# Spreading weight sums, moving stores to ScalarE's queue and low halves to VectorE in a clustered-attention and MLP kernel

## The chip, the cores and the metric

One core of one Trainium2 chip. The time is device microseconds (us) of one execution; lower is better. TensorE multiplies, VectorE (DVE), ScalarE (ACT) and GpSimd (POOL) do elementwise work, SyncE (SP) issues DMAs and computes nothing.

## The reference

Float32 attention whose keys and queries see each other only in the same cluster, and on its output a small mixing MLP:

```
q_assign = argmax(q_n @ c_n.T); k_assign = argmax(k_n @ c_n.T)     # 16 centroids a head
attn = softmax(where(q_assign == k_assign, q @ k.T / 8, -1e9)) @ v # batch 4, heads 8, seq 768, dim 64
x = attn as (4, 768, 512)
u = x + (x^T @ U @ V)^T                                            # rank 32 along seq
out = u + relu(u @ w_ch1) @ w_ch2                                  # 512 -> 2048 -> 512
```

## The kernel before

**Precision.** A float32 operand is split into a high part, rounded to the fast matmul type (a copy, called hi, on ScalarE), and a low part, x - hi (a subtraction, on POOL or DVE). A product is three matmuls: hi x hi, hi x lo, lo x hi. So every operand passes through ScalarE and then POOL or DVE before TensorE can use it.

**Seven products.** The large matrix products use a 2x2 block scheme with seven block products (`products`, line 840) in place of eight. It needs sums of the blocks of weights and activations: s1 to s4 of a weight, t1 to t4 of an activation. `factors`: a11, a12, a22 are raw blocks (three, 768 columns), the four s are sums (1024 columns).

**Stages, in order of time.** To about 444 us: attention. Then the MLP, three kinds of stage:

- *First stage*, 444 to 738 us: 16 groups g (0 to 15), each one batch b and one pair k of eight slices of the hidden layer. Runs: batch 0 k 0 to 3, batch 1 k 0 to 7, batch 0 k 4 to 7. A group has 42 matmuls of 384 columns (`product`, lines 853 to 855, combined on DVE at 861), a Relu on ScalarE (893) and its low half on DVE (891), and 36 matmuls of 512 columns of the second GEMM with plain weights (`gemm2`, 1044 to 1046). On the side the group prepares the next group's weights: `add_w` (819, POOL), `split_w` (829 hi on ScalarE; 827 low, on POOL until group 12's weights, then on DVE), `split_w2` (838 hi; 836 low on POOL); and it joins raw 64-bit weight words (`convert`, 713 to 724; DVE lines 218 to 221).
- *Product stages* of batches 2 and 3 (738 to 809 and 885 to 944): eight groups of 42 matmuls each (g 16 to 31). The weights are read back from memory (`stage_w`, 936) and split (`split_staged`: hi 945, low 943). The Relu results stay in the buffers `h_*` (`relu_home`).
- *Step stages* of batches 2 and 3 (809 to 885, 944 to 1015): the second GEMM, now also by seven products. 56 steps n2 = 8 p + k (product p 0 to 6, k 0 to 7), each six matmuls (`product2`, 994 to 996). A block is eight steps of one p. The activations are split on the way: `split_h` (hi 923, low 921), two k at a time into a ring of four places; `add_h` (914, POOL) makes t1, t2, t4; in batch 2's step stage the u of batch 3 is prepared as well (797 on POOL, 803 and 804). `combine2` (1004 to 1017) adds the blocks, `output` transposes (1027), adds u (1030) and stores (1034). The w2 factors are loaded by `load_w2` (the line of the helper `copy_rows`, 261) into 14 slots; slots 11 to 13 hold the fourth ring place until step 48.

For the step stages, the first stage writes to memory: `keep_sums` (927), the sums of the first weights, 512 KB; `keep_w2` (953), three pieces of 256 KB of split w2; `sums_w2`, per k, eight stages: load 512 KB (963), four sums (968, POOL), hi (970, ScalarE), low (972, POOL), store 1 MB (974). `sums_w2` works in the tile `turned`, which is needed for the blocks of u again from group 14 on.

**Order.** Nothing is scheduled at run time. `at(time, fn, ...)` gives each piece a planned time in units (one product each: a group of the first or the product stage is 7 units, a step is 1); the plan is sorted, and every engine and every DMA queue runs its pieces in that order, waiting on semaphores. So a piece that waits holds what is behind it on its engine, DMA issues too. M0 is the start of group 0, M1 = M0 + 112 that of group 16. Nearly all DMAs are issued by SP.

The placement of the sums, lines 1237 to 1240, and the slots, 976 and 977:

```
for k in range(NK):
    at(M0 + 7 * (k + 4 if k < 4 else k + 8) + 5, keep_w2, k)
    for stage, step in enumerate(phase["sums"]):
        at(M0 + 7 * (k + 5) + step, sums_w2, k, stage)
slots = [n2 % 11 if n2 < 6 * NK else 7 + n2 % NK % 7 for n2 in range(7 * NK)]
slots = {2: slots, 3: slots[:-1] + [0]}
```

Of the kernel before, what the change touches and what calls it, by code (L numbers as in the profile page):

```python
# [51 lines left out]
NK = NF // 2  # L52
# [73 lines left out]
    "sums":    (-2.5, -0.3,  0.1,  0.5,  0.9,  1.4,  1.6,  3.2),  # L126
    "open":    4.5,
    "keep_sums": 0.5,
    "stage":   (-5.0, -3.5),
    "split_w": ( 0.3,  1.2,  1.3,  3.0),  # L130
    "relu":    ( 4.6,  5.6,  6.6,  6.5,  7.4),
    "t1":      10.6,
    "split_h": (-3.8, -2.8),
    "t2":      ( 4.0,  1.8),
    "t4":      (14.5,  2.0),
    "output":  (( 1.2,  1.7,  3.0), ( 2.2,  2.7,  4.0)),
# [26 lines left out]
def clustered_attention_moe(ctx: ExitStack, tc: tile.TileContext, qk, v, cen, moe_U, moe_V, w, out):  # L163
# [752 lines left out]
    def split_h(p, kk, low):  # L916

        x = homes_h[products[p][1]][:, 2 * kk:2 * kk + 2].rearrange("p k q -> p (k q)")
        hi, lo = (ring[kk][:, m] for m in range(2))
        if low:  # L920
            (nc.gpsimd if (4 * p + kk) % 3 == 2 else nc.vector).tensor_sub(lo, x, hi)
        else:
            nc.scalar.copy(hi, x)

    def keep_sums(k):

        nc.sync.dma_start(out=s_scr[k], in_=sums_w)
# [10 lines left out]
    def split_staged(g, part, low):  # L938

        x = staged[g, part].rearrange("p (i c) -> p i c", c=256)  # L940
        hi, lo = (combos[pairs[g][2] % 2][:, 3 * part:3 + 4 * part, m] for m in range(2))
        if low:
            nc.gpsimd.tensor_sub(lo, x, hi)  # L943
        else:
            nc.scalar.copy(hi, x)
# [3 lines left out]
    def keep_w2(k):  # L949

        w2 = live["w2", k % 2]
        for i, (f, c) in enumerate(((0, 0), (1, 0), (1, 256))):
            copy_rows(nc.sync, w2_scr[k][:, i], w2[:, :, f, c:c + 256])
# [3 lines left out]
    def sums_w2(k, stage):  # L957

        x = flat[:, 0:1024]
        pieces = flat[:, 1024:3072].bitcast(F32R).rearrange("p (i m c) -> p i m c", i=4, m=2)  # L960
        if stage == 0:
            assert {(k, 1, 0), (k, 1, 1)} <= stored
            nc.sync.dma_start(out=x, in_=w_scr[k][1])
# [5 lines left out]
        elif stage == 5:  # L969
            nc.scalar.copy(pieces[:, :, 0], x.rearrange("p (i c) -> p i c", i=4))  # L970
        elif stage == 6:
            nc.gpsimd.tensor_sub(pieces[:, :, 1], x.rearrange("p (i c) -> p i c", i=4), pieces[:, :, 0])
        else:
            copy_rows(nc.sync, w2_scr[k][:, 3:7], pieces)

    slots = [n2 % 11 if n2 < 6 * NK else 7 + n2 % NK % 7 for n2 in range(7 * NK)]
    slots = {2: slots, 3: slots[:-1] + [0]}

    def load_w2(b, n):

# [40 lines left out]
    def output(b, p, o, stage):  # L1021
# [223 lines left out]
    def weights_phase(g, m):  # L1245

        for part in range(2):
            at(m + phase["stage"][part], stage_w, g, part)
            for low in range(2):
                at(m + phase["split_w"][2 * part + low], split_staged, g, part, low)  # L1250

    for r, b in enumerate((2, 3)):
# [37 lines left out]
        if r == 0:  # L1290
# [8 lines left out]
            weights_phase(ng + NK, m0 + 14 * NK - 7.8)  # L1299
# [36 lines left out]
```

## Time and profile before

| | |
|---|---|
| time, median of 2 runs | 1022.21 us (1021.65 to 1022.78) |
| profiled execution | 1022.64 us, span 1020.8 us |
| mean granted TensorE clock | 0.975 |
| busy in the span: TensorE, DVE, ScalarE, POOL | 944.5, 768.6, 464.3, 723.4 us |
| DMA moved | 183.14 MB, mean 179 GB/s |

In the rows an engine is PE, DVE, ACT, POOL or SP; a trailing q is its queue of waits and DMA issues. L853 is line 853. "out<-in" names tiles. "<-POOL x L836" is what ended the idle time before. Matmuls overlap, so a busy TensorE is not one at its peak; its granted clock is a share of the full 2.4 GHz, 0.5 being the lower level, 1.2 GHz.

### The profile page before, as it was taken

The page shows a single profiled execution, that of the slowest core. Times are in us where ns is not written, and L with a number is a line of the kernel's source. Part 1 is how long each engine was busy: PE and PEld are TensorE (multiplying, and loading weights), DVE is VectorE, ACT ScalarE, POOL GpSimd, SP SyncE. Part 2 cuts the span into 40 slices and gives each one's busy share as a digit, 9 for nine tenths or more (in the row PEclk, how much of TensorE's full clock was granted, in tenths as well). Part 3 has the DMA queues.
Part 4 walks back from the last instruction along what each step waited for, and adds up shares of the span by engine and source line. Part 5 has one row for each costly group of instructions (what it writes and reads, how often), then busy time and mean ns, then how long its engine had stood idle before and what let it go on. Part 6 is the DMA issues. An engine that isn't in the chain of part 4 may idle for free.

```text
span 1020.8 us, 14867 instructions
## 1 busy us (share of the span) xinstructions
PE 944.5 (93%) x5098; PEld 759.6 (74%) x5098; DVE 768.6 (75%) x1217; ACT 464.3 (45%) x680; POOL 723.4 (71%) x467
## 2 busy tenths in 40 slices
PE   8799999999999999999989779979998969999996
PEld 5466666666667667658877667968898869899895
DVE  5798988778887877568785687665878887687763
ACT  6355555565555545544342433323345543155430
POOL 6467776788678879985787898883647694366950
PEclk8899999999999999999999899999999998999998
DMA  8556656575656674047468665589486956795675
GB/s 204 131 141 165 168 148 187 154 193 145 190 148 183 164 165 104 1 73 228 157 239 293 224 256 183 203 285 259 130 195 164 228 157 194 208 201 173 197 212 126
DMA packets 169646, 183.14 MB, mean 179 GB/s; under 512 B 110426, under 2 KB 119252, under 8 KB 168548
## 3 DMA queue, kind: packets, MB, share of 16 engines
q1 hardware_dynamic: 169056, 182.04, 64.0%
q8 instruction: 40, 0.66, 0.3%
q14 instruction: 34, 0.28, 0.1%
q10 hardware_dynamic: 516, 0.16, 0.1%
HBM read 112.72 MB, written 41.42 MB: 151 GB/s over the span
## 4 chain that ended last, share of the span: by engine, by line
PE 60%; POOL 12%; DVE 11%; DMA 6%; SPq 4%; issue 4%; ACT 3%; ACTq 0%; POOLq 0%; DVEq 0%
PE o_ps L616 12%; PE ps_max L569 6%; PE st L593 6%; PE st L595 5%; PE ps_h L853 3%; PE ps_h L855 3%; PE ps_h L854 3%; SPq L786 3%; POOL h_left L914 3%; PE y L1046 2%; PE y L1045 2%; PE y L1044 2%; POOL turned L968 2%; PE z L995 2%; PE z L994 2%
## 5 line engine op out<-in xcount | busy, mean ns | idle before, releaser
L608 POOL TENSOR_TENSOR T<-T,pr 128x768 f32<-128x768 f32 x120 | 222.7, 1856 | 52.6 <-DVE T L608 30.9
L571 DVE TENSOR_REDUCE m<-ps_max 128x1 f32<-128x384 f32 x372 | 186.7, 546 | 44.9 <-PE ps_max L569 43.4
L598 ACT ACTIVATE pr<-st 128x768 f32<-128x768 f32 x186 | 148.9, 812 | 74.9 <-PE st L595 63.8
L616 PE MATMUL o_ps<-pr,vt 128*64 128x384 f32 x768 | 131.4, 491 | 0.6 <-DMA vt<-in_v 0.2
L853 PE MATMUL ps_h<-arena,combos 128*128 128x384 f32 x352 | 119.8, 340 | 6.9 <-DVE rw_g L861 3.4
L855 PE MATMUL ps_h<-arena,combos 128*128 128x384 f32 x352 | 118.8, 337 | 3.6 <-POOL combos L943 3.6
L569 PE MATMUL ps_max<-arena 128*128 128x384 f32 x372 | 114.8, 375 | 7.5 <-DMA arena<-ohT 5.6
L854 PE MATMUL ps_h<-arena,combos 128*128 128x384 f32 x352 | 118.9, 338 | 0.5 <-DVE arena L804 0.5
L616 PEld LDWEIGHTS o_ps<-pr,vt 128*64 128x64 f32 x768 | 52.4, 137 | 66.6 <-issue 60.8
L593 PE MATMUL st<-arena 128*128 128x384 f32 x372 | 100.1, 350 | 1.3 <-ACT pr L598 1.3
L569 PEld LDWEIGHTS ps_max<-arena 128*128 128x128 f32 x372 | 67.9, 191 | 41.4 <-issue 15.2
L595 PE MATMUL st<-arena 97*128 97x384 f32 x372 | 95.8, 339 | 0.0
L608 POOL TENSOR_TENSOR T<-pr 128x768 f32<-128x768 f32 x30 | 56.5, 1883 | 46.4 <-ACT pr L598 46.4
L1046 PE MATMUL y<-w,hl 128*128 128x512 f32 x192 | 77.8, 405 | 8.1 <-DVE hl L891 7.9
L1045 PE MATMUL y<-w,hh 128*128 128x512 f32 x192 | 77.1, 401 | 6.7 <-POOL w L836 6.7
L853 PEld LDWEIGHTS ps_h<-arena,combos 128*128 128x128 f32 x352 | 66.5, 189 | 14.6 <-issue 4.6
L593 PEld LDWEIGHTS st<-arena 128*128 128x128 f32 x372 | 65.1, 189 | 16.4 <-issue 7.3
L1044 PE MATMUL y<-w,hh 128*128 128x512 f32 x192 | 75.6, 394 | 1.4 <-ACT hh L893 1.4
L893 ACT ACTIVATE hh<-c 128x768 fp32r<-128x768 f32 x32 | 27.0, 845 | 98.8 <-DVE c L861 97.7
L855 PEld LDWEIGHTS ps_h<-arena,combos 128*128 128x128 f32 x352 | 66.5, 189 | 5.2 <-POOL combos L943 5.2
L854 PEld LDWEIGHTS ps_h<-arena,combos 128*128 128x128 f32 x352 | 66.5, 189 | 4.8 <-DVE arena L804 1.0
L595 PEld LDWEIGHTS st<-arena 97*128 97x128 f32 x372 | 68.4, 190 | 0.0
(212 smaller groups left out, 2177.3 us busy)
## 6 DMA issues: line engine op xcount, KB each, us to landing
combos<-w_scr SPq DMA_DIRECT2D x112, 256.0 KB
R<-in_qk SPq DMA_DIRECT2D x32, 384.0 KB
arena<-arena SPq DMA_DIRECT2D x64, 192.0 KB
arena<-arena SPq DMA_DIRECT2D x31, 384.0 KB
late_rw<-in_w SPq DMA_DIRECT2D x20, 512.0 KB
u<-u_scr SPq DMA_DIRECT2D x96, 96.0 KB
w_scr<-turned SPq DMA_DIRECT2D x8, 1024.0 KB
rw<-w_scr SPq DMA_DIRECT2D x15, 512.0 KB
```

The costliest lines, as they stand in the source:

```text
L569: nc.tensor.matmul(ps[:, 0:HS], x1[:, 0, g // 2, g % 2, t * P:(t + 1) * P], x1[:, 1, h, g % 2, :], start=True, stop=True)
L571: nc.vector.reduce_max(live["m2", i][:, h, u:u + 1], ps[:, 0:HS], axis=AX.X)
L593: nc.tensor.matmul(st[:, j, 0:HS], x1[:, 1, hk, j, ks], x1[:, 0, h, j, :], start=True, stop=False)
L595: nc.tensor.matmul(st[:, j, 0:HS], x2[0:97, 1, hk, j, ks], x2[0:97, 0, h, j, :], start=False, stop=True)
L598: nc.scalar.activation(pr, st[:, :, 0:HS], AF.Exp, scale=SCALE)
L608: eng.tensor_add(T, live["p", i, h, 0] if c == 1 else T, live["p", i, h, c])
L616: nc.tensor.matmul(o_ps[64 * j:64 * j + 64, 0:HS], vv[:, c, j, :], pr[:, j, :], start=(c == 0), stop=(c == NT - 1))
L853: nc.tensor.matmul(ps, ah[:, d], oh[:, d], start=(d == 0), stop=False)
L854: nc.tensor.matmul(ps, ah[:, d], ol[:, d], start=False, stop=False)
L855: nc.tensor.matmul(ps, al[:, d], oh[:, d], start=False, stop=(d == 1))
L1045: nc.tensor.matmul(y, hh[:, f, ts], w2[:, 1, f, :], start=False, stop=False)
L1046: nc.tensor.matmul(y, hl[:, f, ts], w2[:, 0, f, :], start=False, stop=(g in lasts and f == 1))
```

## The change

- `sums_w2` no longer stands in groups 5 to 12, one per group, but in groups 5, 7, 8, 10, 11, 13, 14 and 15. Its load is planned four units ahead of the group (2.5 before), its store at 5.0 (3.2 before). For k of 5 and up it works in two tiles of the raw-weight conversion (`late_rw`, `late_g`), and its low half is on DVE.
- `keep_w2` moves by about five units, `keep_sums` by one.
- The DMAs of `keep_sums`, `keep_w2`, the load and the store of `sums_w2`, and the stores of `output` except the last ones of batch 3 are issued by ScalarE. That is 8 + 24 + 8 + 8 + 56 = 104 issues.
- `split_staged`: the low half of part 0 (768 columns) goes from POOL to DVE. `split_h`: all 24 low halves of a step stage on DVE (16 before); planned two units earlier. The stores of `output` are planned two units later.
- Slots of the last block: 7, 8, 9, 10, 6, 11, 12, 13 in both batches (before 7 to 13, and then 7, or 0 in batch 3).
- The first weights of batch 3's product stage are loaded 0.8 units later; the second part is split at -2.6 and -1.5 units before that stage in place of -6.5 and -4.8.

```
 phase = {
-    "sums":    (-2.5, -0.3,  0.1,  0.5,  0.9,  1.4,  1.6,  3.2),
+    "sums":    (-4.0, -0.3,  0.1,  0.5,  0.9,  1.4,  1.6,  5.0),
+    "sums_at": (5, 7, 8, 10, 11, 13, 14, 15),
-    "keep_sums": 0.5,
+    "keep_sums": 1.5,
-    "split_w": ( 0.3,  1.2,  1.3,  3.0),
+    "split_w": ( 0.1,  1.3,  1.1,  2.2),
-    "split_h": (-3.8, -2.8),
+    "split_h": (-5.8, -4.8),
-    "output":  (( 1.2,  1.7,  3.0), ( 2.2,  2.7,  4.0)),
+    "output":  (( 1.2,  1.7,  5.0), ( 2.2,  2.7,  6.0)),
...
-            (nc.gpsimd if (4 * p + kk) % 3 == 2 else nc.vector).tensor_sub(lo, x, hi)
+            nc.vector.tensor_sub(lo, x, hi)
...
-        nc.sync.dma_start(out=s_scr[k], in_=sums_w)
+        nc.scalar.dma_start(out=s_scr[k], in_=sums_w)
...
-            nc.gpsimd.tensor_sub(lo, x, hi)
+            (nc.gpsimd if part else nc.vector).tensor_sub(lo, x, hi)
...
-            copy_rows(nc.sync, w2_scr[k][:, i], w2[:, :, f, c:c + 256])
+            copy_rows(nc.scalar, w2_scr[k][:, i], w2[:, :, f, c:c + 256])
...
-        x = flat[:, 0:1024]
-        pieces = flat[:, 1024:3072].bitcast(F32R).rearrange("p (i m c) -> p i m c", i=4, m=2)
+        if k < 5:
+            x, pieces = flat[:, 0:1024], flat[:, 1024:3072]
+        else:
+            pieces, x = (t.rearrange("p h n -> p (h n)").bitcast(F32) for t in live["late_w"][0:2])
+        pieces = pieces.bitcast(F32R).rearrange("p (i m c) -> p i m c", i=4, m=2)
...
-            nc.sync.dma_start(out=x, in_=w_scr[k][1])
+            nc.scalar.dma_start(out=x, in_=w_scr[k][1])
...
-            nc.gpsimd.tensor_sub(pieces[:, :, 1], x.rearrange("p (i c) -> p i c", i=4), pieces[:, :, 0])
+            (nc.gpsimd if k < 5 else nc.vector).tensor_sub(pieces[:, :, 1], x.rearrange("p (i c) -> p i c", i=4), pieces[:, :, 0])
...
-            copy_rows(nc.sync, w2_scr[k][:, 3:7], pieces)
-    slots = [n2 % 11 if n2 < 6 * NK else 7 + n2 % NK % 7 for n2 in range(7 * NK)]
-    slots = {2: slots, 3: slots[:-1] + [0]}
+            copy_rows(nc.scalar, w2_scr[k][:, 3:7], pieces)
+    slots = [n2 % 11 if n2 < 6 * NK else (7, 8, 9, 10, 6, 11, 12, 13)[n2 % NK] for n2 in range(7 * NK)]
...
+            queue = nc.sync if b == B - 1 and p == 6 else nc.scalar
...
-                nc.sync.dma_start(out=dst[j, :, 12 * side:12 * side + 12, 2 * half + o, :], in_=x[32 * j:32 * j + 32])
+                queue.dma_start(out=dst[j, :, 12 * side:12 * side + 12, 2 * half + o, :], in_=x[32 * j:32 * j + 32])
...
-        at(M0 + 7 * (k + 4 if k < 4 else k + 8) + 5, keep_w2, k)
+        at(M0 + 7 * (k + 5 if k < 4 else k + 9) + 2.9, keep_w2, k)
-            at(M0 + 7 * (k + 5) + step, sums_w2, k, stage)
+            at(M0 + 7 * phase["sums_at"][k] + step, sums_w2, k, stage)
...
-            weights_phase(ng + NK, m0 + 14 * NK - 7.8)
+            weights_phase(ng + NK, m0 + 14 * NK - 7, (-0.6, 0.5, 4.4, 5.5))
```

## Rows read from the trace of the kernel before

**Rows 1.** the page: TensorE's busy time, and the chain that ended last
```profile
PE 944.5 (93%) x5098; PEld 759.6 (74%) x5098; DVE 768.6 (75%) x1217; ACT 464.3 (45%) x680; POOL 723.4 (71%) x467
...
PE 60%; POOL 12%; DVE 11%; DMA 6%; SPq 4%; issue 4%; ACT 3%; ACTq 0%; POOLq 0%; DVEq 0%
```

**Rows 2.** windows: us, busy (instructions) per engine, granted clock, DMA share, GB/s
```profile
533.12:689.54 156.42, 133.08 (x625) 116.29 (x625) 105.33 (x123) 54.34 (x70) 133.95 (x97) 0.95 0.70 244
689.54:705.19 15.65, 15.65 (x79) 14.07 (x79) 7.91 (x12) 5.34 (x7) 6.24 (x6) 1.00 1.06 228
689.54:737.97 48.43, 47.50 (x236) 41.99 (x235) 34.04 (x46) 17.23 (x22) 24.24 (x16) 1.00 0.74 184
750.40:808.77 58.37, 53.92 (x306) 52.63 (x305) 46.39 (x74) 27.72 (x43) 37.88 (x21) 1.00 0.84 192
808.77:847.42 38.65, 29.13 (x145) 27.85 (x145) 35.63 (x25) 15.56 (x22) 36.10 (x16) 0.90 0.62 172
873.39:885.10 11.71, 9.21 (x49) 8.24 (x49) 5.62 (x9) 1.88 (x2) 4.22 (x2) 1.00 1.00 287
944.09:976.02 31.93, 27.67 (x146) 26.40 (x146) 25.84 (x21) 12.47 (x18) 29.63 (x14) 0.95 0.68 194
976.02:1000.98 24.96, 24.96 (x145) 24.96 (x145) 11.91 (x17) 7.54 (x9) 7.30 (x4) 1.00 0.67 200
1000.98:1014.90 13.92, 10.71 (x49) 9.41 (x48) 5.42 (x12) 0.00 (x0) 0.00 (x0) 0.88 0.59 150
```

**Rows 3.** POOL, 533.12 to 689.54, grouped: busy us, mean ns | idle before, releasers
```profile
L968 POOL TENSOR_TENSOR turned<-turned 128x256 f32<-128x256 f32 x32 | 29.8, 932 | 8.5 <-DMA turned<-w_scr 6.6
L972 POOL TENSOR_TENSOR turned<-turned 128x1024 fp32r<-128x1024 f32 x8 | 19.3, 2417 | 9.3 <-ACT turned L970 9.3
```

**Rows 4.** TensorE's waits, 533.12 to 689.54: us in total, times, longest
```profile
PE y L1046 <- DVE hl L891: 7.9, 3, 4.2
PE y L1045 <- POOL w L836: 6.7, 3, 3.4
```

**Rows 5.** TensorE's waits, 808.77 to 847.42
```profile
PE z L995 <- POOL combos L921: 5.2, 1, 5.2
PE z L995 <- POOL arena L921: 4.3, 3, 2.7
```

**Rows 6.** TensorE's waits, 873.39 to 885.10
```profile
PE z L994 <- DMA combos<-w_scr: 2.5, 3, 1.4
```

**Rows 7.** TensorE's waits, 1000.98 to 1020.80
```profile
PE z L994 <- DMA combos<-w_scr: 3.2, 2, 1.6
```

**Rows 8.** tile mT, DMA issues on ScalarE's queue: ns min/median/max, first, last
```profile
L261 ACTq DMA_DIRECT2D arena<-mT x17: 677/732/1287, 36.3 to 417.8; - x17
```

**Rows 9.** timeline of SP, 890 to 1021
```profile
998.94 1.97 SPq L1034 DMA_DIRECT2D out_y<-u  x4
1001.01 2.79 SPq L261 DMA_DIRECT2D combos<-w_scr  x6
```

**Rows 10.** groups of instructions on ScalarE, 533.12 to 689.54
```profile
L970 ACT CAST turned<-turned 128x1024 fp32r<-128x1024 f32 x8 | 8.4, 1052 | 38.7 <-POOL turned L968 38.7
```

**Rows 11.** timeline of DVE, 682 to 740: start us, us, instruction
```profile
683.29 2.82 DVE L827 TENSOR_TENSOR combos<-sums_w,combos 128x1024 fp32r<-128x1024 f32 x1
...
733.33 1.21 DVE L827 TENSOR_TENSOR combos<-sums_w,combos 128x1024 fp32r<-128x1024 f32 x1
```

**Rows 12.** timeline of DVE, 795 to 890
```profile
839.48 5.02 DVE L921 TENSOR_TENSOR arena<-h_t,arena 128x768 fp32r<-128x768 f32 x2
...
857.42 0.95 DVE L921 TENSOR_TENSOR arena<-h_left,arena 128x768 fp32r<-128x768 f32 x1
```

**Rows 13.** timeline of POOL, 795 to 890
```profile
834.48 6.74 POOL L914 TENSOR_TENSOR h_left<-h_left 128x768 f32<-128x768 f32 x3
841.18 2.51 POOL L921 TENSOR_TENSOR combos<-h_left,combos 128x768 fp32r<-128x768 f32 x1
```

**Rows 14.** timeline of ScalarE, 846 to 858
```profile
854.92 0.84 ACT L923 CAST arena<-h_left 128x768 fp32r<-128x768 f32 x1 [0.56 <-PE z L996]
```

More of the change, by code (lines that the diff above doesn't have):

```diff
@@ L971, in sums_w2, with load_w2 @@
         elif stage == 6:
-            nc.gpsimd.tensor_sub(pieces[:, :, 1], x.rearrange("p (i c) -> p i c", i=4), pieces[:, :, 0])
+            (nc.gpsimd if k < 5 else nc.vector).tensor_sub(pieces[:, :, 1], x.rearrange("p (i c) -> p i c", i=4), pieces[:, :, 0])
         else:
-            copy_rows(nc.sync, w2_scr[k][:, 3:7], pieces)
-    slots = [n2 % 11 if n2 < 6 * NK else 7 + n2 % NK % 7 for n2 in range(7 * NK)]
-    slots = {2: slots, 3: slots[:-1] + [0]}
-    def load_w2(b, n):
+            copy_rows(nc.scalar, w2_scr[k][:, 3:7], pieces)
+    slots = [n2 % 11 if n2 < 6 * NK else (7, 8, 9, 10, 6, 11, 12, 13)[n2 % NK] for n2 in range(7 * NK)]
+    def load_w2(n):
         p, k = divmod(n, NK)
-        slot = slots[b][n]
+        slot = slots[n]
         copy_rows(nc.sync, combos[slot // 7][:, slot % 7], w2_scr[k][:, factors2.index(products[p][0])])
     def product2(b, p, k, *tiles):
-        slot = slots[b][NK * p + k]
+        slot = slots[NK * p + k]
         w2 = combos[slot // 7][:, slot % 7]
@@ L1237, in clustered_attention_moe, with weights_phase @@
     for k in range(NK):
-        at(M0 + 7 * (k + 4 if k < 4 else k + 8) + 5, keep_w2, k)
+        at(M0 + 7 * (k + 5 if k < 4 else k + 9) + 2.9, keep_w2, k)
         for stage, step in enumerate(phase["sums"]):
-            at(M0 + 7 * (k + 5) + step, sums_w2, k, stage)
+            at(M0 + 7 * phase["sums_at"][k] + step, sums_w2, k, stage)
     M1 = M0 + 7 * ng
     at(M1 + phase["open"], open_phase)
-    def weights_phase(g, m):
+    def weights_phase(g, m, steps=phase["split_w"]):
         for part in range(2):
@@ L1249, in weights_phase @@
             for low in range(2):
-                at(m + phase["split_w"][2 * part + low], split_staged, g, part, low)
+                at(m + steps[2 * part + low], split_staged, g, part, low)
     for r, b in enumerate((2, 3)):
@@ L1265, in clustered_attention_moe @@
             p, k = divmod(n2, NK)
-            before = [x for x in range(n2) if slots[b][x] == slots[b][n2]]
-            free = before[-1] + 1 if before else 0 if slots[b][n2] > 6 else -7
-            at(m + max(free, n2 - 10.7, 6 * NK if slots[b][n2] > 10 else -7) + 0.3 + 0.02 * n2, load_w2, b, n2)
+            before = [x for x in range(n2) if slots[x] == slots[n2]]
+            free = before[-1] + 1 if before else 0 if slots[n2] > 6 else -7
+            at(m + max(free, n2 - 10.7, 6 * NK if slots[n2] > 10 else -7) + 0.3 + 0.02 * n2, load_w2, n2)
             if b < B - 1 or p < 6:
```

## The prediction

> **What bounds the kernel now.** I read the page first [rows 1]: TensorE is busy 93% of the span, but the chain that ended last is only 60% TensorE; POOL and DVE have 23% of it. So TensorE is the floor, and what the change can touch is the time in which it stands or runs at the lower clock. Next I cut the second half of the span into its stages [rows 2]. One full group of the first MLP stage (7 products and its second GEMM, 78 matmuls) takes 15.65 us when nothing is late. Groups 5 to 12 take 156.42 us for eight, where 8 x 15.65 = 125.2 would do: 31.2 lost. Those are the groups in which the sums of the second weights are made, one per group. Three blocks of eight steps in the last product stage take 24.96 us undisturbed (1.04 us a step); the first three blocks take 38.65 for batch 2 and 31.93 for batch 3: 13.7 and 7.0 lost. The last block takes 11.71 and 13.92 against 8.32: 3.4 and 5.6 lost. All of that is 61 us; the rest of the span the change hardly reaches.
>
> Then I asked in each stage which wait ends last. In groups 5 to 12 POOL is busy 134 of 156 us, and most of its idle time is waiting in mid-chain for ScalarE's cast or a load [rows 2, 3]: its order of work is a loop that is longer than TensorE's. TensorE waits for POOL's low half of w2 and for DVE's low half of the activations [rows 4]. In the step stages it waits for POOL's low halves alone [rows 5], in the last blocks for loads of w2 factors [rows 6, 7].
>
> **The change, part by part.** The sum is made against the profiled execution, 1022.64 us (span 1020.8 and 1.84 around it); the median of the runs is 0.4 below it.
>
> *A. Sums spread, groups 5 to 12.* One sum costs POOL 29.8/8 + 19.3/8 = 6.1 us of work and (8.5 + 9.3)/8 = 2.2 us of waiting in it [rows 3], 8.35 together. Eight stand in these groups before, five after (5, 7, 8, 10, 11): 3 x 8.35 = 25 us leave POOL's loop, 156.4 becomes 131.4, just above TensorE's 125.2. The load four units ahead may also hide the 6.6 us of load waits. Against it: ScalarE now issues DMAs. On its queue one took 0.73 us (0.68 to 1.29) for 6 KB [rows 8]; SP's six 256 KB loads took 0.47 each [rows 9]. I take 0.73, the row on that engine. With three pieces of w2, a load, a store and sometimes the first sums that is 5 x 0.73 = 3.7 us in a group, where ScalarE already waits 38.7 us for POOL in eight groups [rows 10]. A new wait comes with them: the store of the pieces stands until the subtraction is done, and behind it the second Relu, for which DVE's low half and then TensorE wait. Where two sums follow each other (7 and 8, 10 and 11) POOL is still late, and I charge the issues fully: 2 x 3.5 = 7. Gain 25 - 7 = 18; bounds 8 (late in most groups) and 31.
>
> *B. Groups 13 to 15 get three sums.* POOL is busy 24 of 48.4 us there [rows 2], so 3 x 3.7 fit. The subtraction goes to DVE: 1.21 us, or 2.82 beside a busy POOL [rows 11]. The DMA share is 0.74 at 184 GB/s; three loads of 0.5 MB and three stores of 1 MB more make some 270, below the 287 that the last block of batch 2 moved [rows 2]. Cost 2; bounds 0 and 3 x 2.82 = 8.5.
>
> *C. Product stages, batches 2 and 3.* Seven or eight low halves of 768 columns a stage go from POOL to DVE, 0.95 each [rows 12] on a DVE that is busy 46.4 of 58.4 us [rows 2]; POOL's remaining work holds DVE up less. I take 0, bounds -3 (DVE is nearly full) and +1.
>
> *D. Low halves in the steps, all on DVE and two steps earlier.* The rows show a price that depends on the other engine: DVE's 768-column subtraction took 0.95 us with POOL idle and 5.02 for two with POOL working, and POOL's own 2.25 to 2.51 [rows 12, 13]. They take turns, one each per 2.5 us. In the 5.2 us wait, POOL made the needed half only after three differences of h, 834.48 to 841.22 [rows 5, 13]. After the change, steps 3 to 25 (22.9 us) hold for batch 2 ten POOL instructions (4 + 4 differences, 2 of u) and 18 of DVE (12 halves, 4 of u, 2 output additions): ten turns of 2.5 and eight at 0.95 are 32.6 us. A half is planned 4.8 steps ahead of its use, 5.0 - 0.95 = 4.0 us of cover: 32.6 - 22.9 - 4.0 = 5.7 stays lost of 13.7. (The same reckoning before, 14 and 14 with 2.8 steps of cover, gives 10 of the 13.7; the granted clock of 0.90 is in the rest.) Gain 8, bounds 4 and 13.7. Batch 3 has no u to split: eight turns and six at 0.95 are 25.7, covered. I take 5.5 of 7.0, since eight output stores (8 x 0.73 = 5.8 us) now stand between ScalarE's casts, and wait there for DVE's addition; bounds 3 and 7.
>
> *E. Last block, batch 2.* SP no longer stands at the output stores, so the loads go out when the slot is free: up to 3 of the 3.4 [rows 6]. But the second part of the next stage's first weights is now cast at step 53.4 behind four stores: 2.9 + 1.05 (cast [rows 10]) + 2.4 (POOL, 1024 columns [rows 3]) from step 53.1 ends near step 59.2, and is used at step 58. Net gain 1.5, bounds -1 and 3.
>
> *F. Last block, batch 3.* SP issued six loads only at 1001.01, after stores at 998.94 [rows 9], and TensorE waited 3.2 us in two waits, with a clock of 0.88 in this block [rows 2, 7]. Now only three slots are still tied to the end of block five. Gain 3, bounds 1 and 4.5.
>
> Here a rule speaks against the change: the Trainium skill, "DMA: Bandwidth & Descriptors", section "Issuing engines are not separate DMA queues", says that DMAs of all issuing engines run on the same 16 engines, and that a second issuer saves only the time to initiate. The row shows the loads held back at SP itself, before any transfer. By the rule E and F would lose their gains and the sum would be 6 less; by the row they stay.
>
> Sum: 18 - 2 + 0 + 8 + 5.5 + 1.5 + 3 = 34, and 1022.6 - 34 = 989.
>
> **The rivals.** *All stalls go.* POOL's loop stays under TensorE's and ScalarE hides its issues: A 28, B 0, D 21, E 3, F 4.5 make 56.5: 966. For it: a group without a sum runs at 15.65 [rows 2]; against it: five sums still leave POOL's loop at 131.
>
> *The lead is not there, and the loads stay late.* ScalarE's casts already wait for TensorE to free the ring [rows 14], so a cast cannot come earlier. Then D is only the difference in price: POOL's 1024 columns cost twice DVE's (2.42 and 1.21 [rows 3, 11]), so each of some nine halves saves about 0.9, 8 in place of 13.5, and E and F give -1.5 and 3 at most: 18 - 2 + 8 + 1.5 = 25.5, 997. This is the case in which part of the change does not do what it says. By the skill's rule on issuing engines it would be 1000.
>
> *ScalarE takes POOL's place.* Its 104 new issues are 76 us, and each in-order wait for POOL or DVE holds casts and Relus behind it. A falls to 10 and D to 6, the rest is nothing: 1022.6 - 14 = 1008.
>
> *Slower.* The 48 issues of the first stage (48 x 0.73 = 35 us) lie wholly on the way from cast to Relu to TensorE, with POOL's loop as the wait behind them, and A gives nothing: 1022.6 + 35 - 13 = 1045. It decides from 34/11 = 3 us of delay a group on; ScalarE is busy 54 of 156 us there by its casts, so most issues should find it idle.
>
> **How the numbers follow.** Forecast 0.50, all go 0.13, no lead 0.12, ScalarE 0.20, slower 0.05. The time is 989. The forecast's own bounds reach from about 975 to 1003; with the near parts of the others the range is 969 to 1012. A measurement of this kernel tells 2% (20 us, 1001.8) from no change. Faster: nearly all of the first three, 0.73; the same: ScalarE's case and a little of the forecast, 0.22; slower 0.05.
>
> **What would show it.** Right: groups 5, 6, 8, 9, 11 and 12 nearer 15.7 us, with POOL idle in 6, 9 and 12; no low half of h on POOL (line 921); first three blocks near 30 and 26 us; loads for the last block issued before the previous block ends. Wrong: ScalarE's queue waiting for POOL ahead of a Relu, DVE's queue as the releaser in the product stages, the DMA share near 1 in groups 13 to 15, or TensorE standing at the third product of batch 3's first group.

## The result, and the profile after

The changed kernel took 1011.88 us (1011.86 to 1011.91, 2 runs) against 1022.21: ratio 0.9899, 95% interval 0.9856 to 0.9942. The forecast was 989 (969 to 1012): the sign was right, the gain of 10.3 us is a third of the 34 forecast. The profiled execution has a span of 1009.5 us, 11.3 less than before. Cut at the first matmul of each stage, the two traces give:

| stage (term of the forecast) | before | after | gain | forecast |
|---|---|---|---|---|
| up to group 5 | 533.1 | 530.4 | 2.7 | none |
| groups 5 to 12 (A) | 156.4 | 143.7 | 12.7 | 18 |
| groups 13 to 15 (B) | 48.4 | 62.1 | -13.7 | -2 |
| product stage, batch 2 (C) | 70.8 | 73.6 | -2.8 | 0 |
| blocks 1 to 4, batch 2 (D) | 48.0 | 44.8 | 3.2 | 8 |
| last block, batch 2 (E) | 11.7 | 8.3 | 3.4 | 1.5 |
| product stage, batch 3 (C) | 59.0 | 62.0 | -3.0 | 0 |
| blocks 1 to 4, batch 3 (D) | 40.3 | 35.6 | 4.7 | 5.5 |
| last block, batch 3 (F) | 13.9 | 9.9 | 4.0 | 3 |

The gains add up to 11.2 us. Each stage length is of one execution. The start of group 5 lies between 528.8 and 533.5 us in 16 other kernels with nearly the same code up to there, so most of a difference in it can be scatter. But group 4, the last ahead of it, took 19.4 us before and 17.4 in after and in all 16 others: 2.0 of the first 2.7 come with the change, and the forecast had no term for them. It is not the queue, since the 17.4 stay with the early DMAs on SP; what else it is was not parted.

The page of after, its busy line and the engines of the chain that ended last, beside [rows 1]:

```profile
PE 943.9 (93%) x5098; PEld 757.4 (75%) x5098; DVE 781.2 (77%) x1251; ACT 463.8 (46%) x680; POOL 656.8 (65%) x433
...
PE 64%; DVE 13%; POOL 7%; DMA 6%; issue 4%; ACT 3%; SPq 2%; ACTq 1%; POOLq 0%; DVEq 0%
```

POOL lost 67 us of work, DVE took up 13, and the chain has a little less POOL and SP in it. Such a line does not say where 11 us came from. The windows of after do (columns as in [rows 2]): groups 5 to 12; groups 13 to 15; of these, 13, 14 and 15 alone; blocks 1 to 3, block 4 and the last block of batch 2; blocks 1 to 3, block 4 and the last block of batch 3:

```profile
530.44:674.11 143.67, 131.97 (x625) 115.34 (x624) 101.03 (x122) 52.07 (x67) 117.53 (x84) 0.96 0.70 240
674.11:736.20 62.09, 51.92 (x236) 44.84 (x235) 40.61 (x49) 21.62 (x27) 35.70 (x28) 0.93 0.70 215
674.11:689.75 15.64, 15.64 (x79) 13.91 (x79) 10.12 (x13) 5.86 (x7) 9.43 (x10) 1.00 0.99 252
689.75:712.70 22.95, 17.95 (x79) 15.16 (x79) 14.06 (x22) 7.32 (x9) 10.29 (x10) 0.93 0.76 239
712.70:736.20 23.50, 18.33 (x80) 15.77 (x79) 16.42 (x16) 8.44 (x11) 15.99 (x10) 0.89 0.45 168
809.81:839.25 29.44, 26.69 (x145) 24.77 (x145) 29.44 (x22) 14.36 (x20) 24.60 (x11) 1.00 0.68 207
839.25:854.56 15.31, 10.33 (x49) 9.69 (x49) 11.11 (x14) 5.34 (x7) 2.11 (x1) 0.89 0.66 167
871.20:879.52 8.32, 8.32 (x49) 8.32 (x49) 4.91 (x10) 1.02 (x2) 0.00 (x0) 1.00 1.01 316
941.49:966.55 25.06, 25.06 (x146) 24.95 (x145) 25.03 (x20) 11.25 (x16) 21.83 (x9) 1.00 0.76 242
966.55:977.06 10.51, 8.83 (x49) 8.27 (x49) 7.74 (x12) 3.88 (x5) 0.00 (x0) 1.00 0.88 230
993.70:1003.58 9.88, 9.31 (x49) 8.03 (x48) 5.41 (x11) 0.00 (x0) 0.00 (x0) 1.00 0.71 150
```

Group 13 takes the undisturbed 15.6, although a sum stands in it; 14 and 15 take 7.3 and 7.9 us more than that. In blocks 1 to 3 of both batches DVE is busy all the time, and block 4 is slow, which it was not before. TensorE's waits in groups 13 to 15 (0.9 us in all before), and then the longest of DVE and of ScalarE there (columns: us in total, times, longest):

```profile
PE ps_h L854 <- DVE rw_g L862: 5.2, 2, 4.0
PE ps_h L854 <- DVE c L862: 4.6, 2, 4.1
PE y L1050 <- DVE hl L892: 0.4, 1, 0.4
...
DVE turned L793 <- DMA u<-u_scr: 6.9, 2, 5.6
DVE late_rw L976 <- ACT late_rw L974: 6.3, 3, 4.6
...
ACT late_rw L974 <- POOL late_g L972: 7.9, 2, 5.6
```

Read upward, the longest of these are two chains. In group 15 POOL makes the differences of a late sum late; ScalarE's cast (L974) stands 5.6 us at them; DVE's low half (L976) stands 4.6 us at the cast; behind it in DVE's line is the combination (L862) for which TensorE waits 4.1 us. In group 14 DVE's transposes of u stand 5.6 us at their loads, and behind them is the combination for which TensorE waits 4.0 us. The waits are 10.2 us; the rest of the loss goes with the clock: after the two long waits TensorE is granted the lower of its levels, 1.2 in place of 2.4 GHz, for a part of the group (mean 0.93 and 0.89 in these rows, 1.00 in the undisturbed one).

### The profile page after: what moved, and what is told of

The parts are those of the page before. It is cut to its first block, busy times and chain, and to the rows that moved or that the text cites. A ratio compares the mean times of both kernels' runs of the same rounds, so it can differ in the third digit from the quotient of the medians.

```text
span 1009.5 us, 14837 instructions
## 1 busy us (share of the span) xinstructions
PE 943.9 (93%) x5098; PEld 757.4 (75%) x5098; DVE 781.2 (77%) x1251; ACT 463.8 (46%) x680; POOL 656.8 (65%) x433
## 4 chain that ended last, share of the span: by engine, by line
PE 64%; DVE 13%; POOL 7%; DMA 6%; issue 4%; ACT 3%; SPq 2%; ACTq 1%; POOLq 0%; DVEq 0%
PE o_ps L617 12%; PE ps_max L570 7%; PE st L594 6%; PE st L596 6%; PE ps_h L854 4%; PE ps_h L856 4%; PE ps_h L855 4%; PE z L998 3%; PE z L999 3%; PE z L997 3%; PE y L1050 2%; PE y L1049 2%; PE y L1048 2%; POOL sums_w L820 2%; DVE m L572 2%
## 5 line engine op out<-in xcount | busy, mean ns | idle before, releaser
L609 POOL TENSOR_TENSOR T<-T,pr 128x768 f32<-128x768 f32 x120 | 222.7, 1856 | 52.4 <-DVE T L609 30.7
L572 DVE TENSOR_REDUCE m<-ps_max 128x1 f32<-128x384 f32 x372 | 186.5, 545 | 44.8 <-PE ps_max L570 43.2
L854 PE MATMUL ps_h<-arena,combos 128*128 128x384 f32 x352 | 122.3, 348 | 14.1 <-DVE rw_g L862 8.4
L856 PE MATMUL ps_h<-arena,combos 128*128 128x384 f32 x352 | 120.9, 344 | 5.3 <-POOL combos L944 4.0
L855 PE MATMUL ps_h<-arena,combos 128*128 128x384 f32 x352 | 120.6, 343 | 0.5 <-DVE arena L805 0.5
L854 PEld LDWEIGHTS ps_h<-arena,combos 128*128 128x128 f32 x352 | 67.9, 193 | 23.5 <-DVE rw_g L862 9.2
L944 POOL TENSOR_TENSOR combos<-rw,combos 128x1024 fp32r<-128x1024 f32 x10 | 24.9, 2490 | 92.7 <-ACT combos L946 92.7
L594 PEld LDWEIGHTS st<-arena 128*128 128x128 f32 x372 | 65.1, 189 | 16.4 <-issue 7.3
L856 PEld LDWEIGHTS ps_h<-arena,combos 128*128 128x128 f32 x352 | 67.8, 192 | 7.6 <-POOL combos L944 5.7
L855 PEld LDWEIGHTS ps_h<-arena,combos 128*128 128x128 f32 x352 | 68.1, 193 | 4.6 <-DVE arena L805 1.0
```

The lines of the kernel that those rows point to most:

```text
L572: nc.vector.reduce_max(live["m2", i][:, h, u:u + 1], ps[:, 0:HS], axis=AX.X)
L594: nc.tensor.matmul(st[:, j, 0:HS], x1[:, 1, hk, j, ks], x1[:, 0, h, j, :], start=True, stop=False)
L609: eng.tensor_add(T, live["p", i, h, 0] if c == 1 else T, live["p", i, h, c])
L854: nc.tensor.matmul(ps, ah[:, d], oh[:, d], start=(d == 0), stop=False)
L855: nc.tensor.matmul(ps, ah[:, d], ol[:, d], start=False, stop=False)
L856: nc.tensor.matmul(ps, al[:, d], oh[:, d], start=False, stop=(d == 1))
```

## The experiments

Each run was compared with the kernel before on the same chip; ratios are to it, with 95% intervals. "Groups 13 to 15" and the like are stages as in the table. Kernels that share a stage's code agree within a few us there: groups 5 to 12 of nine kernels with after's code took 142.6 to 146.4.

**Sums at 5 to 12 again.**

```
-    "sums_at": (5, 7, 8, 10, 11, 13, 14, 15),
+    "sums_at": (5, 6, 7, 8, 9, 10, 11, 12),   # old times, tile and engine of the sums
```

> The changed kernel, with the sums of the second weights alone as before: one in each of groups 5 to 12, in the tile turned, low half on POOL, old load and store times; the moved queues and all else stay. Theory (the spread carries the gain of groups 5 to 12 and the loss of 13 to 15): groups 13 to 15 fall from 62.1 to about 48.5 us, groups 5 to 12 rise from 143.7 to about 153, so 1006 to 1010 in all against 1011.9. Rival (SP's relief, not the spread, made the gain of groups 5 to 12): they stay near 144, and the whole is about 998.

Measured 1017.24 us, ratio 0.9956 (0.9935 to 0.9978). Groups 5 to 12 took 157.4, groups 13 to 15 52.1. The direction is the theory's, but both stages and the total lie above it. So the spread gives 13.7 in A and takes 10.0 in B; the moved queues without the spread make nothing of A's gain (157.4 against 156.4 before). What they add to the spread is read from the early DMAs on SP, below. B stays 3.6 above before without any sum in it.

**Low half of the late sums on POOL.**

```
-            (nc.gpsimd if k < 5 else nc.vector).tensor_sub(pieces[:, :, 1], ...
+            nc.gpsimd.tensor_sub(pieces[:, :, 1], ...
```

> The changed kernel, with one edit: the low half of the sums of k = 5 to 7 (groups 13 to 15) is made on POOL in place of DVE. Theory (DVE stands in order at that low half until POOL's sums and ScalarE's cast are done, 4.6 us in group 15, and TensorE's 4.05 us wait is the end of it): group 15 falls from 23.5 to about 19.5 us, group 14 little, total about 1008. Rival (the three sums' volume of work and transfers is what costs): no change within 1 us, 1011 to 1013.

Measured 1014.39, ratio 0.9921 (0.9894 to 0.9949); groups 13 to 15 61.7, group 15 23.2: the rival's. ScalarE's cast still stood 5.6 us at POOL's differences; DVE now stood at the casts of the next weights, which follow on ScalarE, and TensorE waited 5.5 us in place of 4.1 for a combination behind them. DVE's low half is not a needed link of the chain.

**Late DMAs on SP.**

```
-            nc.scalar.dma_start(out=x, in_=w_scr[k][1])
+            (nc.scalar if k < 5 else nc.sync).dma_start(out=x, in_=w_scr[k][1])   # store and keep_w2 likewise
```

> The changed kernel, with the DMAs of the late groups alone issued by SP again: the w2 pieces of k = 4 to 7 and the loads and stores of the sums of k = 5 to 7. Theory (ScalarE's queue runs beside SP's and slows the block reads of u, 16.7 us for eight against 6 to 8 before, so that DVE's transposes wait 5.6 us in group 14): reads take about 8 us per eight again, group 14 falls from 22.95 to 17 to 19 us, total 1006 to 1008. Rival (the bytes, not the queue): reads stay late, group 14 above 21, total 1011 or more.

Measured 1017.01, ratio 0.9937 (0.9911 to 0.9963); groups 13 to 15 61.2, the next stage 77.7 against 73.6. Group 14 took 22.6, the rival's time, but not for the rival's reason. The second eight reads of u, as SP issued them in before, in after and in this run:

```profile
699.28 5.95 SPq L786 DMA_DIRECT2D u<-u_scr  x8
...
684.81 16.72 SPq L787 DMA_DIRECT2D u<-u_scr  x8
...
685.46 4.28 SPq L787 DMA_DIRECT2D u<-u_scr  x8
```

With the late DMAs on SP, behind the reads, the reads are quick, as the theory said, and DVE no longer stands at them. In their place the sum's own transfers are late, and TensorE waits the same 4.0 us in group 14:

```profile
DVE late_rw L976 <- ACT late_rw L974: 5.7, 1, 5.7
...
ACT late_rw L974 <- DMA w_scr<-late_rw: 7.2, 1, 7.2
```

So the queue decides which of the two is late; moving the DMAs back takes next to nothing off the loss.

**Late sums, copies only.**

```
+        elif k >= 5 and 1 <= stage <= 6:
+            pass                               # and x is stored twice in place of pieces
```

> The changed kernel, but of the three late sums (groups 13 to 15) the arithmetic is left out (four differences on POOL, the cast on ScalarE, the low half on VectorE); the load of 0.5 MB stays and the same 1 MB is stored, from the tile as loaded, so the sums of the last three rows of the second weights are not computed. Theory (the arithmetic of the sums is put in line on three in-order engines and holds up casts, joins and combinations behind it): groups 13 to 15 fall from 62.1 to about 52 to 53 us, as without sums, and the time to about 1002. Rival (traffic: 4.5 MB more beside the reads of u and of the weights): they stay at 60 to 62 us and the time at 1011 to 1013.

Measured 1004.23, ratio 0.9807 (0.9782 to 0.9831). **Late sums not stored:** load and arithmetic kept, `elif k < 5:` ahead of the store.

> The changed kernel with loads and arithmetic of the three late sums kept and their 1 MB stores left out (the step stages then load the pieces of three rows earlier in their place, so as many bytes, but not the reference's values). Theory (arithmetic in line): groups 13 to 15 stay at 59 to 62 us, because what goes is only the issue of a store behind a wait. Rival (traffic, or the next sum's cast waiting for the store out of the same tile): 54 to 57 us, time 1005 to 1007.

Measured 1012.07, ratio 0.9876 (0.9847 to 0.9905). **Late sums without POOL:** only their four differences left out.

> The changed kernel with the four differences on POOL of each of the three late sums left out (so these sums hold the plain weights); load, cast on ScalarE, low half on VectorE and store stay. Theory (the price is POOL's 4 to 4.5 us a sum, which pushes its low halves and its differences of u beside VectorE's work): groups 13 to 15 fall from 62 to 52 to 55 us, time 1002 to 1005. Rival (the cast and the low half in the line, which wait and are waited for): they stay at 58 to 62 us, time 1008 to 1012.

Measured 1005.81, ratio 0.9846 (0.9818 to 0.9874). The windows of groups 13 to 15 in these three, in this order:

```profile
678.96:730.39 51.43, 48.22 (x235) 41.73 (x234) 33.92 (x45) 17.45 (x22) 23.82 (x15) 1.00 0.77 232
```

```profile
673.96:735.69 61.73, 51.46 (x236) 44.38 (x236) 40.57 (x49) 21.00 (x26) 35.71 (x28) 0.94 0.58 163
```

```profile
676.69:731.54 54.85, 48.57 (x235) 41.63 (x234) 38.58 (x48) 20.01 (x25) 24.85 (x15) 1.00 0.76 234
```

The theory held in the last two, and the first came just under its 52 to 53. Arithmetic gone and bytes kept: 10.7 us back, with more GB/s than after's 215. Stores gone and arithmetic kept: 0.4 back, though the DMA share fell from 0.70 to 0.58. Of the 10.7, POOL's differences are 7.2, the cast and the low half 3.4.

**Reads of u half a group earlier.**

```
-                at(m + 1 + h, fetch_blocks, pairs[g + 3][1], h)
+                at(m + h - (2.5 if g > 7 else -1), fetch_blocks, pairs[g + 3][1], h)
```

> The changed kernel with the eight strided reads of batch 2's rows of u planned 3.5 products earlier (about 8 us), in the middle of group 12. Theory (the wait of 5.6 us at VectorE for these reads is what TensorE pays in group 14, 4.0 and 1.3 us): group 14 falls from 22.9 to 17.5 to 18.5, groups 13 to 15 from 62.1 to 57 to 58, time about 1007. Rival (the transfers are crowded wherever they lie, or VectorE is late there by its own order): groups 12 to 15 together change by less than 1.5 us.

Measured 1009.54, ratio 0.9861 (0.9834 to 0.9888). Group 14 fell from 22.9 to 17.9, groups 13 to 15 to 57.9: as the theory said. Group 15 took 24.4 (23.5 in after).

**Late sums later in their group** (with the earlier reads).

```
+            step = step if k < 5 else (-1.2, 1.9, 2.2, 2.5, 2.8, 4.3, 5.4, 6.5)[stage]
```

> The changed kernel with the earlier reads of u (as in the run of that alone) and the arithmetic of the three late sums planned later in its group: load at -1.2 products, differences at 1.9 to 2.8, cast at 4.3, low half at 5.4, store at 6.5, in place of -4.0, -0.3 to 0.9, 1.4, 1.6 and 5.0. The same work, the same queues. Theory (the price of a late sum is its cast and its low half standing in line ahead of the next group's weight casts and of combinations while POOL is late with the differences): groups 13 to 15 fall from 57.9 to 50 to 54 us, time 1002 to 1006. Rival (it is the work itself, POOL's 4.5 us and what it slows on VectorE): they stay at 56 to 60 us, time 1007 to 1011; then only fewer sums there help.

Measured 1010.53, ratio 0.9876 (0.9834 to 0.9917). Groups 13 to 15 took 55.8, outside the theory's 50 to 54 and just below the rival's range; the next stage took 76.5 in place of 73.5, so nothing was won. Here another place in the line moved the work's price and did not remove it.

**Early DMAs on SP.**

```
-            nc.scalar.dma_start(out=x, in_=w_scr[k][1])
+            (nc.sync if k < 5 else nc.scalar).dma_start(out=x, in_=w_scr[k][1])   # other early DMAs likewise
```

> The changed kernel with the DMAs of groups 4 to 12 (pieces of w2, first sums, loads and stores of the five early sums) on SP's queue again, at their new places. The forecast charged 7 us to their issue on ScalarE. Theory (that charge was right): groups 5 to 12 fall from 143.7 to 137 to 139 us, time 1005 to 1007. Rival (the issues lie in ScalarE's idle time, and POOL's line with the cast in its middle is what is left): they stay at 142.5 to 146.5 us, the spread of six kernels with the same code there, time 1009 to 1014.

Measured 1019.05, ratio 0.9966 (0.9945 to 0.9986). Both were wrong: groups 5 to 12 rose to 150.8, and 4 of the 7 us lie in groups 7 and 8 (41.0 in place of 36.9). POOL's differences there, first in this kernel, then in after, beside [rows 3] (columns: busy us, mean ns, idle before and its releasers):

```profile
L972 POOL TENSOR_TENSOR turned<-turned 128x256 f32<-128x256 f32 x20 | 19.4, 970 | 7.8 <-DMA turned<-w_scr 6.6
```

```profile
L972 POOL TENSOR_TENSOR turned<-turned 128x256 f32<-128x256 f32 x20 | 19.2, 961 | 1.2
L976 POOL TENSOR_TENSOR turned<-turned 128x1024 fp32r<-128x1024 f32 x5 | 12.7, 2531 | 8.7 <-ACT turned L974 8.7
```

On SP the sums' loads are waited for 6.6 us, as before; on ScalarE they are not. Of the 6.6, 5.9 are one load, that of group 8's sum. SP stood 8.5 us for one of DVE's joins at a load of raw weights (L714) ahead of it; in after (last line) ScalarE issued the same load some 9 us earlier, counted from the group's start:

```profile
SPq L714 <- DVE joined L222: 13.8, 2, 8.5
...
584.86 0.81 SPq L714 DMA_DIRECT2D late_rw<-in_w  x2
...
588.55 0.83 SPq L967 DMA_DIRECT2D turned<-w_scr  x1
...
576.90 0.34 ACTq L967 DMA_DIRECT2D turned<-w_scr  x1
```

So A's 12.7 us need both: the spread without the moved queue gives 5.6 (156.4 to 150.8), the moved queue without the spread -1.0.

**Early sums, copies only:** as for the late ones, for k < 5.

> The changed kernel with the arithmetic of the five early sums (groups 5, 7, 8, 10, 11) left out, as was done with the three late ones; their loads stay, and as many bytes are stored. Theory (a sum costs TensorE less than the 8.35 us of POOL that the forecast put on it, and what is lost in these groups is also other work, the joins and halves of group 6 first): groups 5 to 12 fall from 143.7 to 130 to 136 us. Rival (the forecast's: what is lost is all POOL's line of the sums): 125 to 128 us, the 125.2 of undisturbed groups.

Measured 993.21, ratio 0.9724 (0.9697 to 0.9752). Groups 5 to 12:

```profile
529.96:655.86 125.90, 125.68 (x626) 112.15 (x625) 87.94 (x122) 47.34 (x63) 83.08 (x60) 1.00 0.79 275
```

The rival held: 125.9 against 125.2 undisturbed. All that groups 5 to 12 still lost came from the five sums, 17.8/5 = 3.6 us each.

**Output stores on SP.**

```
-            queue = nc.sync if b == B - 1 and p == 6 else nc.scalar
+            queue = nc.sync
```

> The changed kernel, with all output stores of the step stages issued by SP again, at their new, later places. Theory (on ScalarE a store waits in order for DVE's addition and holds the casts behind it): the fourth blocks fall from 15.3 to about 9.5 us and from 10.5 to 8.4, the first product groups of batch 3 lose their 2.4 us of stalls, but the last blocks rise by some 3 us each since the loads stand behind the stores again: in all 1007 to 1009. Rival (DVE's own order is what is late): the fourth blocks stay above 14 and 10, and the total is 1014 to 1018 because the last blocks get worse.

Measured 1012.2 (1009.9 to 1015.8), ratio 0.9906 (0.9872 to 0.9939). The product stage of batch 3 took 59.0 again, its first three groups 7.3 each in place of 8.4, 8.8 and 8.0. The last block of batch 2 took 9.5, that of batch 3 9.9 as in after, but what follows it to the end of the span took 8.1 in place of 6.0. Block 4 stayed at 15.3 in batch 2 and at 10.3 in batch 3. The theory held for the product stage, the rival for block 4.

**Lead back to 3.8 and 2.8 steps**, low halves still on DVE: `"split_h": (-3.8, -2.8)`.

> The changed kernel with the splits of h again 3.8 and 2.8 steps ahead, in place of 5.8 and 4.8; the low halves stay on VectorE. Theory (both parts count: a step is 1.04 us, so two steps of cover are 2 us in each of the waits): the first three blocks go from 29.4 to 32 to 34 us in batch 2 and from 25.0 to 27 to 29 in batch 3, time 1016 to 1020. Rival (the engine alone does it, since the casts cannot come earlier than the ring is free): both stages stay within 1 us, time 1011 to 1013.

Measured 1015.72, ratio 0.9920 (0.9896 to 0.9943). Blocks 1 to 3 took 36.4 and 29.1 us (29.4 and 25.1 in after), but block 4 only 9.3 and 8.8 (15.3 and 10.5). The theory's direction held for the three blocks, which rose by more than it said; over four the lead is worth 0.9 in batch 2 and 2.3 in batch 3.

**Four edits**: sums at 12, 13, 14; the earlier reads; stores of batch 2's blocks 6 and 7 on SP; and

```
+                    t += 8 * (p == 1)          # output of block 2 (p = 1), eight steps later
```

> The changed kernel with four edits, each read in its own stage: the late sums at groups 12, 13, 14 in place of 13, 14, 15; the reads of batch 2's u 3.5 products earlier; the output stores of the last two blocks of batch 2 on SP; the output of block 1 (transpose, addition, store) eight steps later, in block 3 in place of block 2. Theory (each loss is work put in line ahead of work that TensorE needs): groups 12 to 15 go from 78.5 to 68 to 72 us, since the last sum no longer stands beside POOL's two differences of u; the fourth block of batch 2 from 15.3 to 11 to 12, since 3.9 us of VectorE work no longer stand ahead of its halves; the product stage of batch 3 from 62.2 to 59 to 60; time 995 to 1001. Rival (a sum costs its 6 us of POOL wherever it lies, and the fourth block waits for the turns that VectorE and POOL take): groups 12 to 15 stay at 73 to 75, the fourth block at 14 to 15.5, time 1003 to 1006.

(Its block 1 is p = 1, the second block.) Measured 1006.21, ratio 0.9844 (0.9819 to 0.9869). Groups 12 to 15 took 73.2: the rival's, a sum costs about as much in group 12. Block 4 fell to 12.8, near the theory, but block 5 rose from 8.3 to 12.9; the product stage of batch 3 took 61.0: its first four groups took the undisturbed 7.3 us each, but group 28 took 8.8, as it did not in after. The time lies between the two.

**The same without that last edit.**

> The changed kernel with three edits that have each been seen to help: reads of batch 2's u 3.5 products earlier, late sums at groups 12, 13, 14, output stores of the last two blocks of batch 2 on SP; the outputs of block 1 stay where the change put them. Theory (the gains add, and the later output of block 1 only moved a wait from the fourth block to the fifth): groups 12 to 15 at 73 to 74 us, blocks 1 to 6 of batch 2 at 61.4 again (63.4 with the later output), product stage of batch 3 at 60 to 61, time 1003.5 to 1006. Rival (the waits that are taken away come back in the next stage): time 1007 to 1010.

Measured 1004.69, ratio 0.9826 (0.9802 to 0.9850): groups 12 to 15 73.2, blocks 1 to 6 61.4, product stage of batch 3 59.2. The gains add.

**Differences of all sums on DVE** (on top of it): `nc.vector.tensor_tensor` for them.

> The kernel with the three good edits (reads of u earlier, late sums at 12, 13, 14, output stores of batch 2's last blocks on SP), and the four differences of all eight sums on VectorE in place of POOL. Estimated from rows: 256 columns take about 0.35 us on VectorE (384 take 0.55, 768 take 0.95), 1.4 a sum, against 3.6 to 4.3 on POOL. Theory (the price is POOL, the slower engine whose line the weights' halves wait in): groups 5 to 12 fall from 146 to 130 to 137 us, groups 13 to 15 from 53.7 to 50 to 52, time 986 to 996. Rival (any arithmetic in line costs it, and VectorE stands nearer to TensorE than POOL): groups 5 to 12 stay at 143 to 148, time 1002 to 1007, or slower.

Measured 1006.11, ratio 0.9830 (0.9802 to 0.9858). Groups 5 to 12 took 146.7, the rival's, groups 13 to 15 51.0, the theory's.

**The early low halves on DVE too:** `nc.vector.tensor_sub` for every k.

> As the run before it, and the low half of the five early sums on VectorE too (1.21 us alone against 2.41 on POOL). Theory (POOL's time is the price): groups 5 to 12 fall by 1 to 5 us more, to 127 to 134, time 983 to 994. Rival (VectorE, busy 101 of 144 us there before these 16 us, now ends last): they rise against the run before it by 1 to 6 us.

Measured 999.75 (997.75 to 1002.33), ratio 0.9771 (0.9748 to 0.9794): 2.3% faster than before and faster than every other version here that computes the reference; after's own ratio is 0.9899. The sums are no longer on POOL at all. Windows of groups 5 to 12 and 13 to 15:

```profile
528.83:675.74 146.91, 133.91 (x625) 116.77 (x624) 112.51 (x153) 53.57 (x69) 87.99 (x59) 0.94 0.69 245
675.74:726.28 50.54, 48.46 (x235) 42.21 (x234) 40.43 (x54) 18.93 (x24) 23.62 (x15) 0.99 0.81 234
```

In groups 13 to 15 the engine was the price: 3.1 us less than with the sums on POOL. In groups 5 to 12 POOL is busy 88 of 147 us in place of 121, and they take no less: the rival of the run before held there, and neither side of this one (146.7 to 146.9). Another 1.5 of the 4.9 us to the run with three edits lie ahead of group 5, in the scatter. Of the 6.4 us to the run before, the two traces show 3.6, and 3.4 of these lie ahead of group 5, where the kernels do not differ: what the early low halves on DVE gave is not shown. One of the two waits of 4 us that are left, in this kernel's ScalarE and DVE (start us, us, instruction, idle before it):

```profile
551.82 1.05 ACT L830 CAST combos<-sums_w 128x1024 fp32r<-128x1024 f32 x1 [4.61 <-POOL sums_w L820]
...
553.51 0.66 ACT L716 ACTIVATE late_g<-late_rw 128x512 f32<-128x512 f32 x1
...
554.20 1.62 DVE L219 TENSOR_SCALAR joined<-late_g 128x512 int32<-128x512 int32 x1 [2.04 <-ACT late_g L716]
555.85 2.77 DVE L220 SCALAR_TENSOR_TENSOR joined<-late_g,joined 128x512 int32<-128x512 int32 x1
558.65 2.71 DVE L222 SCALAR_TENSOR_TENSOR joined<-late_rw,joined 128x512 int32<-128x512 int32 x1
561.29 0.55 DVE L862 TENSOR_TENSOR rw_t<-ps_h,rw_g 128x384 f32<-128x384 f32 x1
```

A chain like that of group 15 in after: POOL's first sums, ScalarE's line, DVE's line (three joins of the raw weights), and last the combination that TensorE stands at. Why it still runs late in groups 6 and 8 with so little on POOL was not settled.

## Why the prediction was wrong, point by point

**B is the step that failed**, "POOL is busy 24 of 48.4 us there [rows 2], so 3 x 3.7 fit": 13.7 lost, beyond the bound of 8.5. A mean busy share over three groups was read as free time where the work was put. POOL's idle time there is waiting in mid-chain, in after 9.9 us for DVE's halves and 7.6 for ScalarE's casts, and in group 15 POOL is busy 16 of 23.5 us (three differences of u stand there too). Without the arithmetic of the sums the three groups take 10.7 us less: a sum costs TensorE 10.7/3 = 3.6 us there, as much as in groups 5 to 12 (31.2/8 = 3.9 by [rows 2], 3.6 by the run without them). The other 3.0 are there without the arithmetic too (3.6 with the sums at 5 to 12). The late reads of u are in them: DVE stands 4.0 us at them in group 14 of that run. Earlier reads gave 4.2 back, which in part is the same loss, since group 14 fell to 18.4 us without the arithmetic and to 17.9 with the earlier reads. Of the traffic, which I checked against 287 GB/s, the bytes were not the price: 3 MB fewer gave 0.4. (My sum there comes to 277 GB/s, not 270.) But beside the DMAs moved to ScalarE's queue the reads of u were late (16.7 us for eight, 4.3 with the late DMAs back on SP), and for that the forecast had no term.

**A was mis-sized by the same mistake turned round**: 12.7 for 18. I took 3 x 8.35 us of POOL out of one long loop. But POOL's time is not TensorE's: a sum cost TensorE 3.9 on the mean, and three are 11.7. That quotient stood in [rows 2]. A and B together are -1: the spread moved the loss. The mean hides that the groups do not pay alike: before the change groups 7 and 10 took 15.6 and 15.7 us with a sum in each. Of the groups named as signs, 9 and 12 came to 15.6 and 16.4 and 5, 8 and 11 only to 17.6 to 18.6, but group 6 took 22.5 with no sum in it (first row): it pays for the sums of others, since it fell to 16.1 without their arithmetic (second row).

```profile
548.44:570.94 22.50, 18.41 (x79) 16.35 (x79) 18.01 (x18) 6.02 (x8) 19.52 (x16) 0.85 0.68 240
...
545.60:561.74 16.14, 15.92 (x79) 13.81 (x78) 12.41 (x15) 5.41 (x8) 11.18 (x8) 1.00 0.90 337
```

The charge of 7 for issues on ScalarE had the wrong sign: with them on SP these groups take 7 longer. The rival "ScalarE takes POOL's place" fell with it in these groups. That its 1008 was nearest is luck: what it describes showed only in C of batch 3, and it has neither B's loss of 13.7 nor the gains of E and F. (The 13 in the rival "Slower" is added up nowhere.)

**C** was charged nothing and cost 5.8. In batch 3 it is 3.0, the price of the moved output stores. Those of blocks 6 and 7 of batch 2, four at a time, stand on ScalarE's queue ahead of and between the casts and copies of the next stage:

```profile
877.16 2.07 ACTq L1038 DMA_DIRECT2D out_y<-u  x4
879.33 1.05 ACT L946 CAST combos<-rw 128x1024 fp32r<-128x1024 f32 x1 [3.66 <-PE z L999]
...
889.42 2.99 ACTq L1038 DMA_DIRECT2D out_y<-u  x4
892.45 0.52 ACT L902 ACTIVATE arena<-c 128x384 fp32r<-128x384 f32 x1 [2.19 <-DMA out_y<-u]
```

An issue took 0.52 to 0.75 us in these rows (0.73 forecast from [rows 8]). I had put this wait into E, where it takes the 3 down to 1.5, and looked no further than its first group; the sign named for it came (TensorE stood 0.8 us at the third product of batch 3's first group), but the three groups lost 1.1, 1.5 and 0.7. With the stores on SP all of it is gone. Of the 2.8 in batch 2, one wait of 1.2 us is for a low half that the change moved to DVE (L944); no run took the rest apart.

**D**: blocks 1 to 3 did better than forecast in batch 2 (29.4 where 38.65 - 8 = 30.7 was forecast) and reached the undisturbed 25 in batch 3 with DVE busy 25.03 of 25.06 us. But I cut the stage at block 3, and the backlog came out in block 4: 6.0 and 2.2 us. DVE ahead of it, and TensorE's wait, in after:

```profile
828.68 5.97 DVE L922 TENSOR_TENSOR arena<-h_left,arena 128x768 fp32r<-128x768 f32 x3
834.58 1.01 DVE L1007 TENSOR_TENSOR c<-z,z 128x384 f32<-128x384 f32 x2
835.51 1.67 DVE L922 TENSOR_TENSOR combos<-h_left,combos 128x768 fp32r<-128x768 f32 x1
837.10 0.57 DVE L1030 STREAM_TRANSPOSE c<-c 128x384 f32<-128x384 f32 x1
837.60 2.10 DVE L805 TENSOR_TENSOR arena<-turned,arena 128x768 fp32r<-128x768 f32 x1
839.62 2.15 DVE L1033 TENSOR_TENSOR u<-c,u 128x384 f32<-128x384 f32 x1
841.69 0.57 DVE L1030 STREAM_TRANSPOSE c<-c 128x384 f32<-128x384 f32 x1
842.29 0.56 DVE L1033 TENSOR_TENSOR u<-c,u 128x384 f32<-128x384 f32 x1
842.77 1.82 DVE L922 TENSOR_TENSOR arena<-h_t,arena 128x768 fp32r<-128x768 f32 x2
...
PE z L998 <- DVE arena L922: 6.4, 3, 4.2
```

Not a gap in DVE's line up to the half for which TensorE stands 4.2 us. The reckoning in turns of DVE and POOL was about right (three halves took 5.97 us beside POOL, 0.95 each [rows 12] alone); its window was too short. The Trainium skill, "SBUF — State Buffer", section "Who interferes with whom", names a reason: DVE's second port pair is shared with GpSimd under an exclusive lock. The rows agree, 2.0 against 0.95. The rival "the lead is not there" fell: without it blocks 1 to 3 are 7.0 and 4.0 us longer, though block 4 takes back 6.1 of the 7.0.

**E and F** came by more than the forecast, 3.4 and 4.0 (bounds -1 to 3 and 1 to 4.5; the new cast charged to E is C's loss). No load is waited for in the last block of batch 2, and beside the 3.2 us of [rows 7] there stands now:

```profile
PE z L997 <- DMA combos<-w_scr: 0.5, 2, 0.3
```

But my reason, SP standing at the stores, was the smaller part of it: with all stores back on SP at their later places F kept its whole gain and E 2.2 of 3.4, and the end behind F's block took 2.1 longer. What is left for the rest is the new slots and the later stores; no run parts the two. The Trainium skill's rule that issuing engines are not separate queues ("DMA: Bandwidth & Descriptors", section "Issuing engines are not separate DMA queues"), by which both gains would have gone, is borne out here only as far as the queue by itself did little; the loads came early all the same. In groups 5 to 12 the measurement goes against it: 143.7 us with two issuing queues, 150.8 with one.

## What to carry to other kernels

Before moving work to where an engine has idle time, divide the loss of the old place by the number of pieces, and look what the idle engine waits for at the new place: idle time in the middle of a chain across in-order engines is not free. When work is given a lead, follow the backlog to the first stretch in which the engine idles again, and end the sum there. Price a moved DMA by what stands behind it on the new queue and by what stood ahead of it on the old one.

## What the runs showed that was not expected

A second issuing queue paid although the DMAs and their bytes were the same: with 6.6 us less waiting for the sums' loads, eight groups ran 7 us faster. In group 14 the same queue made the reads of u late. A single wait of 4 us costs TensorE more than 4: group 15 lost 7.9 us with 5.2 of waits, at a granted clock of 0.89. And with 33 us of POOL's work gone from groups 5 to 12 these took the same time, 146.9 against 146.3.
